# A retention layer with a gated convolution on one core: queries of six batches loaded four tokens to a partition, keys and queries turned apart, one load queue, and a new order in the slot

## The chip, the cores and the metric

The kernel runs on one NeuronCore of a Trainium2 chip. The metric is the device time of one execution in microseconds. PE is the matrix engine, DVE the vector engine, ACT the scalar engine, POOL the GpSimd engine and SP the sync engine, which here only issues transfers. SBUF is the on-chip memory, PSUM the small memory that PE writes; here PSUM is full, with eight banks of 2 KB per partition all in use.

## The reference

```python
def _attn_ref(q, k, v):                      # q, k, v: (8, 8, 576, 64) float32
    B, H, S, D_ = q.shape
    scores = 1.0 / np.sqrt(D_) * np.matmul(q, k.transpose(0, 1, 3, 2))
    gamma = 1.0 - 2.0 ** (-5.0 - np.arange(H, dtype=np.float32))
    rel = np.arange(S)[:, None] - np.arange(S)[None, :]
    Dmat = np.where(rel >= 0, gamma[:, None, None] ** rel[None, :, :], 0.0)
    return np.matmul(scores * Dmat[None], v)

def _moe_ref(x, w_val, conv_w, w_out):       # x: (8, 576, 512); conv_w: (5, 512)
    K = conv_w.shape[0]
    xp = np.concatenate([np.zeros((B, K - 1, D), np.float32), x], axis=1)
    gate_pre = sum(conv_w[k][None, None, :] * xp[:, k:k + S, :] for k in range(K))
    gate = 1.0 / (1.0 + np.exp(-gate_pre))
    return ((gate * (x @ w_val)) @ w_out).astype(np.float32)
```

The result of the attention, with the heads put side by side, is the `x` of the second part. There is no softmax: the decay `gamma ** (i - j)` splits into a factor for the key and one for the query, so a running state of keys times values can stand for all earlier tokens.

## The kernel before

**Tiling.** A batch has 576 tokens: four full chunks of 128 and a tail of 64. The list `chunks` holds 36 of them: for each group of four batches, sixteen full chunks, and then two tail chunks which pair the tails of two batches. Two chunks that follow each other make one unit of 256 tokens, and there are 18 units.

**One chunk.** `load` brings k, q and v by three transfers of 256 KB from SP, 64 floats (256 bytes) at a piece. `cast` on POOL makes bfloat16 copies `kb`, `qb` and, multiplied by the key's decay factor, `vb`. `turn` (L199) transposes `kb` and `qb` by PE into one PSUM tile `tps`, of which there is one; DVE copies the keys out (`kt`, L208), ACT the queries (`qt`, L209). `scores` (L220) multiplies them per head into two PSUM tiles, `masks` (L229) applies the causal mask on DVE, `values` (L261) multiplies with `vb`, on top of what `carried` (L244) has put there from the running state, and `take_x` (L270) scales the result by the query's factor into `xg`. `update` (L289) adds the chunk's keys and values to the state in PSUM, and `take_state` (L300) copies it out on ACT for the next chunk.

**One unit.** `conv` (L322) is 40 small matmuls with diagonal weights, `gate` (L330) two sigmoids on ACT, `value` two sets of 8 matmuls (L337), each with a product by the gate on DVE (`z`, L340), and `project` two sets of 4 matmuls (L347), each with a copy on ACT (`ob`, L350) and a transfer to the result from SP. These six PSUM tiles take turns in three banks, `g`.

**Order.** Nothing is reordered by a scheduler: each engine's instructions stand in the order in which the code is run through, with semaphores between engines. The loop runs over slots t = -2 to 37. Slot t loads chunk t+6, casts chunk t+4, turns chunk t+2, makes the scores of chunk t+1 and the values of chunk t. An even slot also runs `conv`, `gate` and `value` of unit t/2 - 1, the following odd slot its `project`. An engine thus waits at the first instruction whose input is not there, with all that is behind it. At most nine chunks of loads and four of casts are held at a time. The weights are loaded by ACT's queue, while SP loads the first chunks.

Of the kernel before, what the change touches and what calls it, by code (L numbers as in the profile page):

```python
# [13 lines left out]
F32 = mybir.dt.float32  # L14
# [7 lines left out]
def kernel(  # L22
# [20 lines left out]
    LA = 8  # L43
    assert D == 64 and DM == H * D and TAIL == 64 and B % GB == 0 and NP == 4
# [9 lines left out]
    op_sb = ctx.enter_context(tc.tile_pool(name="osb", bufs=3))  # L54
# [15 lines left out]
    with tc.manual_schedule():  # L70
# [3 lines left out]
        def load_chunk(b, c):  # L74
            for name, src in (("k", k), ("q", q), ("v", v)):
                t = half.tile([P, H, D], F32, name=f"f{name}c", bufs=LA + 1)
                nc.sync.dma_start(out=t, in_=src[b, :, c * P:(c + 1) * P, :].rearrange("h p d -> p h d"))  # L77
                loaded[name, "full", b, c] = t

        def load_tail(b):  # L80
            for name, src in (("k", k), ("q", q), ("v", v)):
                t = half.tile([P, H, D], F32, name=f"f{name}c", bufs=LA + 1)
                for i in range(2):
                    nc.sync.dma_start(out=t[i * TAIL:(i + 1) * TAIL],
                                      in_=src[b + i, :, NCH * P:S, :].rearrange("h p d -> p h d"))
                loaded[name, "tail", b, NCH] = t

        def load(t):
            kind, b, c = chunks[t]
            if kind == "full":  # L90
                load_chunk(b, c)
            else:
                load_tail(b)

        load(0)
        load(1)

        cwn = consts.tile([KC * NP, P], F32, name="cwn")
        nc.scalar.dma_start(out=cwn, in_=moe_conv_w.rearrange("k (o i) -> (k o) i", i=P))
        wvf = consts.tile([P, NP, DM], F32, name="wvf")  # L100
        wof = consts.tile([P, NP, DM], F32, name="wof")
        nc.scalar.dma_start(out=wvf, in_=moe_w_val.rearrange("(o i) n -> i o n", i=P))
        load(2)
        wo_src = moe_w_out.rearrange("(pr ab hl p) n -> ab hl p pr n", pr=2, ab=2, hl=2)
        for (p0, blk, ab, hl) in ((0, 0, 0, 0), (64, 0, 1, 0), (0, 2, 1, 1), (64, 2, 0, 1)):
            nc.scalar.dma_start(out=wof[p0:p0 + 64, blk:blk + 2, :], in_=wo_src[ab, hl])
# [3 lines left out]

        ident = consts.tile([P, P], BF16, name="ident")
# [3 lines left out]
        identf = consts.tile([32, 32], F32, name="identf")  # L115
        nc.vector.tensor_copy(identf, ident[0:32, 0:32])
# [5 lines left out]
        mask_t = consts.tile([P, P], BF16, name="maskt")  # L122
        nc.vector.tensor_copy(mask_t, mask)
        nc.vector.memset(mask_t[0:64, 64:128], 0.0)

        lrow = consts.tile([P, H], F32, name="lrow")
        lcol = consts.tile([P, NP], F32, name="lcol")
        for h in range(H):
# [302 lines left out]
```

## Time and profile before

| | us |
|---|---|
| median of 3 runs (range) | 194.98 (194.31 to 196.57) |
| the profiled execution | 196.09 |
| its span, first to last instruction | 194.1 |
| start of `conv` of unit 0, 2 and 16 | 29.29, 49.98, 178.22 |
| PE busy in the span | 152.2 (78%) |
| DVE, ACT, POOL busy | 114.3, 89.3, 86.9 |
| read from memory, written to it | 30.42 MB, 9.44 MB |

The profile tells for one execution when each engine worked, and what ended each idle time. It has three parts: a start until unit 2, in which data arrive; fourteen units from 49.98 to 178.22 that look alike; and an end, in which the last two units run without new chunks. The groups of instructions give a mean duration, which serves as the price of one instruction. The chain of waits goes back from the last instruction to what released it. The profiled execution took 1.1 us more than the median, of which 2.0 us lie outside the span.

### The profile page before, as it was taken

Reading aid. Unit: us, or ns where it says so; the run is one execution under the profiler, and the core shown is the slowest. Engines: PE = TensorE matmul, PEld = TensorE weight load, DVE = VectorE, ACT = ScalarE, POOL = GpSimd, SP = SyncE. Lnnn points to the kernel's source line nnn. Section 1 sums busy time; section 2 is a strip of 40 time slices with the busy share of each in tenths; the row PEclk is TensorE's granted clock in tenths of the full one; section 3 lists DMA queues with packets and bytes.
Section 4 is the critical chain, followed back from the end, with each engine's and each line's share of the span. In section 5 each row is a group of like instructions: output and inputs, shape, how many; then the busy total and the mean of one; then the engine's idle time right before and its main releaser. Section 6 shows DMA issues by size and latency. Waiting matters only on the chain.

```text
span 194.1 us, 5639 instructions
## 1 busy us (share of the span) xinstructions
PE 152.2 (78%) x2273; PEld 111.0 (57%) x2273; DVE 114.3 (59%) x211; ACT 89.3 (46%) x183; POOL 86.9 (45%) x126
## 2 busy tenths in 40 slices
PE   0112666998898989898988899788989898979990
PEld 0001545775666676667766576666666666667740
DVE  6406774747475657575766657474766575747420
ACT  0072635354646454444435464446463535354431
POOL 8214685655454626453644534454445362520000
PEclk9999999699999999999999999999999999999997
DMA  5999999999999999799999795999997998931124
GB/s 136 287 205 163 220 223 182 234 221 200 256 250 238 247 230 255 158 243 216 277 193 281 169 282 127 231 231 280 233 237 187 245 253 187 237 142 62 52 105 108
DMA packets 118919, 40.21 MB, mean 207 GB/s; under 512 B 113242, under 2 KB 113262, under 8 KB 118894
## 3 DMA queue, kind: packets, MB, share of 16 engines
q1 hardware_dynamic: 117760, 37.76, 86.3%
q10 hardware_dynamic: 1134, 2.11, 4.2%
q8 instruction: 17, 0.28, 0.7%
q14 instruction: 8, 0.07, 0.1%
HBM read 30.42 MB, written 9.44 MB: 205 GB/s over the span
## 4 chain that ended last, share of the span: by engine, by line
PE 48%; DMA 18%; ACT 12%; DVE 9%; SPq 4%; issue 4%; POOL 1%; ACTq 0%; DVEq 0%; POOLq 0%
PE g L337 10%; PE g L347 9%; PE g L322 9%; DMA fvc<-in_v_dram 7%; ACT qt L209 6%; DMA out_dram<-ob 5%; DMA fkc<-in_k_dram 5%; PE tps L205 5%; PE s L220 5%; PE o L261 4%; ACT gate L330 4%; PE st L289 4%; DVE kt L208 4%; DVE p L229 3%; SPq L77 2%
## 5 line engine op out<-in xcount | busy, mean ns | idle before, releaser
L229 DVE TENSOR_TENSOR p<-s,mask 128x512 bf16<-128x512 f32 x64 | 43.7, 684 | 19.3 <-PE s L220 19.3
L337 PE MATMUL g<-xg,wvb 128*128 128x256 bf16 x288 | 37.1, 272 | 14.7 <-ACT gate L330 13.4
L193 POOL TENSOR_TENSOR vb<-fvc,gin 128x512 bf16<-128x512 f32 x36 | 37.5, 1043 | 22.2 <-DMA fvc<-in_v_dram 16.0
L340 DVE TENSOR_TENSOR z<-gate,g 128x512 bf16<-128x512 f32 x36 | 24.8, 688 | 33.4 <-ACT gate L330 24.7
L337 PEld LDWEIGHTS <-wvb 128*128 128x128 bf16 x288 | 27.3, 97 | 21.1 <-issue 18.3
L191 POOL CAST kb<-fkc 128x512 bf16<-128x512 f32 x36 | 22.9, 636 | 31.9 <-DMA fkc<-in_k_dram 21.1
L192 POOL CAST qb<-fqc 128x512 bf16<-128x512 f32 x36 | 22.2, 617 | 29.4 <-DMA fqc<-in_q_dram 29.2
L347 PE MATMUL g<-wob,z 128*128 128x512 bf16 x144 | 34.4, 380 | 0.3 <-DVE z L340 0.3
L209 ACT COPY qt<-tps 128x512 bf16<-128x512 bf16 x36 | 21.1, 585 | 26.8 <-DVE kt L208 25.6
L350 ACT COPY ob<-g 128x512 f32<-128x512 f32 x36 | 21.0, 589 | 19.7 <-DMA out_dram<-ob 14.1
L300 ACT CAST sbd<-st 64x256 bf16<-64x256 f32 x48 | 17.6, 367 | 25.2 <-PE st L289 24.7
L322 PE MATMUL g<-xg,dg 64*64 64x256 bf16 x720 | 23.2, 271 | 0.0
L208 DVE COPY kt<-tps 128x512 bf16<-128x512 bf16 x36 | 15.1, 421 | 11.8 <-PE tps L205 11.7
L270 DVE TENSOR_TENSOR xg<-o,gout 128x512 bf16<-128x512 f32 x32 | 21.8, 681 | 0.0
L347 PEld LDWEIGHTS <-z 128*128 128x128 bf16 x144 | 13.3, 99 | 13.7 <-DVE z L340 1.2
L205 PE MATMUL tps<-ident,kb 128*128 128x128 bf16 x144 | 14.9, 229 | 7.1 <-POOL kb L191 7.1
L330 ACT ACTIVATE gate<-g 128x512 f32<-128x512 f32 x36 | 19.6, 601 | 1.7 <-PE g L322 1.7
L322 PEld LDWEIGHTS <-dg 64*64 64x64 bf16 x720 | 18.4, 106 | 2.0 <-issue 0.4
L205 PE MATMUL tps<-ident,qb 128*128 128x128 bf16 x144 | 14.9, 229 | 5.7 <-POOL qb L192 5.7
L220 PE MATMUL s<-qt,kt 64*128 64x128 bf16 x288 | 15.0, 225 | 4.5 <-ACT qt L209 4.3
L220 PEld LDWEIGHTS <-kt 64*128 64x128 bf16 x288 | 10.1, 96 | 10.2 <-DVE kt L208 4.1
L261 PE MATMUL o<-p,vb 128*64 128x128 bf16 x288 | 15.4, 230 | 0.0
(45 smaller groups left out, 108.1 us busy)
## 6 DMA issues: line engine op xcount, KB each, us to landing
fkc<-in_k_dram SPq DMA_DIRECT2D x32, 256.0 KB, 5.0
fqc<-in_q_dram SPq DMA_DIRECT2D x32, 256.0 KB, 5.3
fvc<-in_v_dram SPq DMA_DIRECT2D x32, 256.0 KB, 4.8
out_dram<-ob SPq DMA_DIRECT2D x32, 256.0 KB, 3.8
wvf<-in_moe_w_val_dram ACTq DMA_DIRECT2D x1, 1024.0 KB, 9.7
wof<-in_moe_w_out_dram ACTq DMA_DIRECT2D x4, 256.0 KB, 10.5
fkc<-in_k_dram SPq DMA_DIRECT2D x8, 128.0 KB, 3.4
fqc<-in_q_dram SPq DMA_DIRECT2D x8, 128.0 KB, 3.3
```

Of the source, the lines that this page charges most:

```text
L191: nc.gpsimd.tensor_copy(kb, loaded["k", kind, b, c])
L193: nc.gpsimd.tensor_tensor(vb, loaded["v", kind, b, c], gin[:, c, :].unsqueeze(2).to_broadcast([P, H, D]), op=ALU.mult)
L205: nc.tensor.transpose(ps[:, i, pr, :], flat[:, pr * P:(pr + 1) * P], ident)
L209: nc.scalar.copy(qt, ps[:, 1])
L220: nc.tensor.matmul(s[i][:, pr, :], lhsT=kt[r, pr, :], rhs=qt[r, pr, :], start=(pr == 0), stop=(pr == NP - 1), skip_group_check=True)
L229: nc.vector.tensor_tensor(p, sps[t][i], m.unsqueeze(1).to_broadcast([P, NP, P]), op=ALU.mult)
L261: nc.tensor.matmul(o[r, pr, :], lhsT=vb[:, 2 * pr + i, :], rhs=pt[t, i][:, pr, :], start=(fresh and pr == 0), stop=(pr == NP - 1), skip_gr ...
L322: nc.tensor.matmul(g[bank][cols, pr, :], lhsT=dg[rows, blk, kk, :], rhs=xs(n, rows, blk, kk), start=(pr == 0 and kk == 0), stop=(pr == 1 a ...
L330: nc.scalar.activation(t, gps[n][i], AF.Sigmoid)
L337: nc.tensor.matmul(vps[:, j, :], lhsT=wvb[:, o, 2 * i + j, :], rhs=xs(n, slice(0, P), o, PAD), start=(j == 0 and o == 0), stop=(j == 1 and ...
L340: nc.vector.tensor_tensor(z, gsb[n][i], vps, op=ALU.mult)
L347: nc.tensor.matmul(o, lhsT=zsb[n, j // 2][:, j % 2, i * P:(i + 1) * P], rhs=wob[:, j, :], start=(j == 0), stop=(j == NP - 1))
```

## The change

It has five pieces.

1. Of batches 2 to 7, the queries of the four full chunks come by one transfer of 1 MB (`load_queries`). Partition p holds tokens 4p to 4p+3, so that a piece is 1024 bytes long. A transposition of one of the four token positions r gives 128 columns for tokens r, r+4, r+8 and so on. ACT writes them with a step of four elements into a tile `qtb` of the whole batch, in which they stand in token order again. The queries of batches 0 and 1 and of all tails are loaded as before ("own").
2. `turn` is split into `turn_k` and `turn_q`, each with its own PSUM tile of half the size, from the same single buffer. A table `qjobs` deals the query jobs to slots: an own job two slots ahead of its chunk, a batch's four jobs one by one to the free slots before the batch begins. Slots 2, 3 and 4 hold two jobs each, and slots 29 to 31 and 34 onwards none. `cast_q` stands two slots ahead of its `turn_q`.
3. The weights `wvf` and `wof` move to SP's queue, between chunks 1, 2 and 3; ACT's queue keeps only the small `cwn`.
4. The constants before the loop are made in another order and partly on other engines: the zeroing of `sbd`, `sbl` and `xg` moves from POOL to DVE, `mask_t` from DVE to POOL into slot 2, the first two casts of k to DVE. The table for the sigmoid is loaded ahead by a one-column `warm`, and the diagonals and `wob` are made in four pieces each.
5. The order in a slot is new: `take_state` comes first, the two `gate` right behind `conv`, `turn_q` between the two halves of `value` or `project`, and `update` of the next chunk at the end. In odd slots `take_x` and the second mask come behind the copy of the keys. `ob` has five buffers instead of three.

The core of the diff:

```diff
-    op_sb = ctx.enter_context(tc.tile_pool(name="osb", bufs=3))
+    op_sb = ctx.enter_context(tc.tile_pool(name="osb", bufs=5))
...
+        def load_queries(b):
+            t = half.tile([P, H, RQ, D], F32, name="fqb", bufs=2)
+            nc.sync.dma_start(out=t.rearrange("p h r d -> p h (r d)"),
+                              in_=q[b, :, 0:RQ * P, :].rearrange("h (p r) d -> p h (r d)", r=RQ))
+            loaded["qb", b] = t
...
-        nc.scalar.dma_start(out=wvf, in_=moe_w_val.rearrange("(o i) n -> i o n", i=P))
+        nc.sync.dma_start(out=wvf, in_=moe_w_val.rearrange("(o i) n -> i o n", i=P))
...
+        def turn_q(job, eng=None):
+            ps = turned(qbf[job])
+            if job[0] == "own":
...
+                b, r = job[1:]
+                if r == 0:
+                    qtd["batch", b] = tp_sb.tile([P, NP, RQ * P], BF16, name="qtb", bufs=2)
+                dst = qtd["batch", b].rearrange("p o (n r) -> p o r n", r=RQ)[:, :, r, :]
+            if eng is nc.vector:
+                nc.vector.tensor_copy(dst, ps)
+            else:
+                nc.scalar.copy(dst, ps)
...
+            for b in qload.get(t, []):
+                load_queries(b)
             if t >= 0 and ok(t + LA - 2):
                 load(t + LA - 2)
+            for job in qjobs.get(t + 2, []):
+                cast_q(job)
             if ok(t + 4):
-                cast(t + 4)
+                cast_kv(t + 4)
+            if ok(t):
+                take_state(t)
             if ok(t + 1):
                 scores(t + 1)
                 masks(t + 1, 0)
             if ok(t):
                 values(t)
-                take_x(t)
-            if ok(t + 1):
+                if not odd:
+                    take_x(t)
+            if ok(t + 1) and not odd:
                 masks(t + 1, 1)
             if unit and not odd:
                 conv(n)
...
+                gate(n, 0)
+                gate(n, 1)
             if ok(t + 2):
-                turn(t + 2)
+                turn_k(t + 2)
+            if ok(t) and odd:
+                take_x(t)
+            if ok(t + 1) and odd:
+                masks(t + 1, 1)
...
+            if unit:
+                project(n, 0) if odd else value(n, 0)
+            for i, job in enumerate(jobs):
+                if i == 1 and unit:
+                    project(n, 1) if odd else value(n, 1)
+                turn_q(job, nc.vector if t < 0 else None)
+            if unit and len(jobs) < 2:
+                project(n, 1) if odd else value(n, 1)
             if ok(t + 1):
                 carried(t + 1)
+                update(t + 1)
```

The table `qload` puts the transfers of the batches 2 and 3 into slots 0 and 1, ahead of the loads of chunks 6 and 7, and those of batches 4 to 7 into slots 5, 11, 15 and 19.

How the instructions move is seen at three places. The first is ACT in slots 20 and 21 (unit 9), before. `sbd` and `sbl` are the copies of the state, `qt` or `qtb` the turned queries, `ob` the result's tile.

```order
L300 CAST sbd_187<-st 64x4x64 x2
L209 COPY qt<-tps 128x512
L330 ACTIVATE gate_2310<-g 128x512
L330 ACTIVATE gate_2312<-g 128x512
L300 CAST sbl_189<-st 64x4x64 x2
L209 COPY qt<-tps 128x512
L350 COPY ob<-g 128x512 x2
```

The same stretch of the changed kernel:

```order
L340 CAST sbd_184<-st 64x4x64 x2
L370 ACTIVATE gate_2321<-g 128x512
L370 ACTIVATE gate_2323<-g 128x512
L244 COPY qtb<-tps 128x512
L340 CAST sbl_186<-st 64x4x64 x2
L390 COPY ob<-g 128x512
L244 COPY qtb<-tps 128x512
L390 COPY ob<-g 128x512
```

The queries' copy stood ahead of the two gates; it now stands behind both, and in the odd slot between the two result copies.

The second place is DVE in slot 13 and the even slot 14, before: masks `p`, the taking of `xg`, the keys' copy `kt`, and the products `z`.

```order
L229 TENSOR_TENSOR p_1558<-s_1548,mask 128x512
L270 TENSOR_TENSOR xg_199<-o,gout 128x4x128
L229 TENSOR_TENSOR p_1569<-s_1549,mask 128x512
L208 COPY kt<-tps 128x512
L229 TENSOR_TENSOR p_1633<-s_1623,mask 128x512
L270 TENSOR_TENSOR xg_199<-o,gout 128x4x128
L229 TENSOR_TENSOR p_1644<-s_1634,mask 128x512
L208 COPY kt<-tps 128x512
```

And in the changed kernel, the same two slots:

```order
L269 TENSOR_TENSOR p_1595<-s_1585,mask 128x512
L227 COPY kt<-tps 128x512
L310 TENSOR_TENSOR xg_196<-o,gout 128x4x128
L269 TENSOR_TENSOR p_1613<-s_1586,mask 128x512
L269 TENSOR_TENSOR p_1668<-s_1658,mask 128x512
L310 TENSOR_TENSOR xg_196<-o,gout 128x4x128
L269 TENSOR_TENSOR p_1679<-s_1659,mask 128x512
L227 COPY kt<-tps 128x512
```

In the odd slot the keys' copy moved from the end to behind the first mask; in the even slot it stays behind both masks.

The third place is POOL at the casts of chunks 4 and 5, before; the numbers tell the tiles apart (`fkc_129` and `fkc_135` hold the keys of chunks 4 and 5):

```order
L191 CAST kb_288<-fkc_129 128x512
L192 CAST qb_289<-fqc_131 128x512
L193 TENSOR_TENSOR vb_290<-fvc_133,gin_175 128x512
L191 CAST kb_349<-fkc_135 128x512
L192 CAST qb_350<-fqc_137 128x512
L193 TENSOR_TENSOR vb_351<-fvc_139,gin_175 128x512
```

And in the changed kernel, where `fqb_290` is the tile of batch 2's queries:

```order
L212 CAST qb_298<-fqc_131 128x512
L212 CAST qb_300<-fqb_290 128x512
L197 CAST kb_302<-fkc_129 128x512
L198 TENSOR_TENSOR vb_303<-fvc_133,gin_164 128x512
L212 CAST qb_366<-fqc_137 128x512
L212 CAST qb_368<-fqb_290 128x512
L197 CAST kb_370<-fkc_135 128x512
L198 TENSOR_TENSOR vb_371<-fvc_139,gin_164 128x512
```

The cast of the first quarter of batch 2's queries (`fqb`, which needs the 1 MB transfer) now stands ahead of the cast of chunk 4's keys.

196 lines of the change are left out of this document (116 added, 80 removed).

## The prediction

> **What bounds the kernel now.** I read first the page's head and its queues, to see which resource could be full, then the busy time by stretches, with the stretches cut at the starts of `conv` of units 2 and 16, and then the waits within the long middle stretch.
>
> ```profile
> span 194.1 us, 5639 instructions
> q1 hardware_dynamic: 117760, 37.76, 86.3%
> q10 hardware_dynamic: 1134, 2.11, 4.2%
> PE 48%; DMA 18%; ACT 12%; DVE 9%; SPq 4%; issue 4%; POOL 1%; ACTq 0%; DVEq 0%; POOLq 0%
> ```
>
> Two things are nearly full: the transfers (the queues' packets fill 86.3 + 4.2% of the 16 engines' time) and PE, which leads the chain of waits with 48%. The stretches say which of the two sets the pace. Their columns are length, busy time of PE, PEld, DVE, ACT and POOL, the granted PE clock, the transfers' share and GB/s.
>
> ```profile
> 34.00:58.20 24.20, 22.17 (x300) 15.98 (x300) 15.32 (x26) 11.45 (x26) 13.84 (x19) 0.93 1.11 232
> 49.98:178.22 128.24, 114.52 (x1777) 84.74 (x1780) 81.54 (x143) 64.15 (x137) 59.57 (x79) 1.00 0.93 219
> 178.22:194.10 15.88, 10.62 (x146) 6.85 (x144) 5.05 (x10) 4.70 (x9) 0.00 (x0) 0.94 0.33 100
> ```
>
> The middle stretch holds 14 units in 128.24 us, 9.16 us each. PE is busy for 114.52 of it, 8.18 us a unit, and idle for 13.7 us. The transfers' share is 0.93, 119.3 us. Who ends PE's idle time there (total us, times, longest):
>
> ```profile
> PE g L337 <- ACT gate L330: 10.5, 14, 0.8
> PE s L220 <- ACT qt L209: 1.8, 6, 0.5
> PE g L337 <- ACT ob L350: 1.1, 2, 0.8
> ACT ob L350 <- DMA out_dram<-ob: 14.1, 11, 2.5
> ```
>
> Three waits make 13.4 of the 13.7 us. The chain through one unit shows them in place (start, length, what).
>
> ```profile
> 58.30 0.40 PE s L220 x8
> 58.69 0.34 PE o L261 x8
> 59.04 1.22 PE g L322 x40
> 60.59 0.46 PE tps L205 x8
> 61.07 0.44 DVE kt L208
> 61.53 0.59 ACT qt L209
> 62.12 0.51 ACT gate L330
> 62.66 1.03 PE g L337 x8
> 64.92 0.45 PE tps L205 x8
> 65.37 1.73 PE g L347 x8
> 67.10 0.22 PE o L244 x4
> 67.35 0.40 PE s L220 x8
> ```
>
> The second half of `value` needs the bank that the first gate empties. That gate stands behind the queries' copy, and that behind the keys' copy: it ends at 62.6, 2.4 us after `conv` has ended at 60.26. An undisturbed unit takes 67.35 - 58.30 = 9.05 us. PE and its partners set the pace; loads delay it only now and then, where `ob` waits for its transfer.
>
> **The new order in the slot.** The prices of what stands beside PE:
>
> ```profile
> L229 DVE TENSOR_TENSOR p<-s,mask 128x512 bf16<-128x512 f32 x64 | 43.7, 684 | 19.3 <-PE s L220 19.3
> L340 DVE TENSOR_TENSOR z<-gate,g 128x512 bf16<-128x512 f32 x36 | 24.8, 688 | 33.4 <-ACT gate L330 24.7 <-PE g L337 8.7
> L270 DVE TENSOR_TENSOR xg<-o,gout 128x512 bf16<-128x512 f32 x32 | 21.8, 681 | 0.0
> L208 DVE COPY kt<-tps 128x512 bf16<-128x512 bf16 x36 | 15.1, 421 | 11.8 <-PE tps L205 11.7
> L209 ACT COPY qt<-tps 128x512 bf16<-128x512 bf16 x36 | 21.1, 585 | 26.8 <-DVE kt L208 25.6
> L350 ACT COPY ob<-g 128x512 f32<-128x512 f32 x36 | 21.0, 589 | 19.7 <-DMA out_dram<-ob 14.1 <-issue 4.6 <-PE g L347 0.8
> ```
>
> I walk once through two slots with the new order. PE's pieces from the chain: scores 0.40, values 0.34, `conv` 1.22, one transposition 0.23 (half of 0.46), half a `project` 0.86, half a `value` as much (8 matmuls of 256 columns against 4 of 512), `carried` and `update` 0.22 each. The even slot takes 0.40 + 0.34 + 1.22 + 0.23 + 0.86 + 0.23 + 0.86 + 0.44 = 4.58 us, the odd slot, without `conv`, 3.36, the pair 7.94.
>
> Who would be late? After `conv`, at 1.96, ACT has nothing ahead of the gates, so the first ends at about 1.96 + 0.55; `value`'s second half starts at 3.28, and the wait of 10.5 us in 14 is gone. On DVE in the even slot the first mask can start at 0.47, then 0.684 + 0.681 + 0.684 + 0.421 put the keys' copy at 2.94; the queries' transposition, which needs the same `tps`, is due at 3.05. In the odd slot, the product `z` of the slot before ends 0.25 in, the mask starts at 0.47, and the copy ends at 1.57, against 1.83. The spare time is thus 0.1 and 0.26 us: enough, but thin. The queries' copy in the even slot ends near 3.9, long before the next transposition. It is also no longer what the next scores wait for, as a batch's queries are turned slots ahead: the 1.8 us go. With five `ob` the copy has two more transfers' time, and the 1.1 us go. The masks are due before the next scores by 0.4 us.
>
> The copy into `qtb` writes with a step of four elements, which no row shows. From below, it is the 0.585 of the plain copy; from above, I take twice that. Both lie beside PE: in the even slot it would end at 4.5, and the next transposition starts at 5.3. I take 0.585.
>
> So the pace falls to between 8.05 us (9.05 less the waits of 0.76 and 0.25 in the chain's unit) and the 8.18 of PE's busy time, and I add a little for new handoffs: 8.22. Over 14 units 115.0, a gain of 13.2 us. Bounds: 15.5 (8.05), and for the other end see the transfers.
>
> **The transfers.** The mean packet of q1 takes 0.863 x 16 x 194.1 / 117760 = 22.8 ns; nearly all are of 256 bytes. One of q10, mostly of 2 KB, takes 0.042 x 16 x 194.1 / 1134 = 115 ns. A packet of 1 KB is in no row. By bytes between these two it takes 62 ns; bounds are 57 (half of 115) and 91 (four small ones). About 22 of the 24 batched chunks' queries load in the middle stretch: 22 x 1024 x 22.8 / 16 = 32.1 us of the 119.3, which become 21.9. That leaves 109.1, under PE's 115.0. At 91 ns it stays 119.3, above it; that is a rival. The page "DMA: Bandwidth & Descriptors" of the Trainium skill (section "Why small descriptors are slow") gives a 256-byte piece 11 cycles, 3 of them overhead, so that 1 KB would save a fifth, not the third taken here; by it, as an estimate, a packet would take 72 ns, the middle stretch would still fit, and the 1 MB transfer in the start would cost 0.6 us more. No row here shows which holds.
>
> POOL casts as much as before. The transfer of batch 4's queries waits on SP until POOL has cast batch 2's last quarter, with chunk 11's loads queued behind; that cast stands one slot earlier, and chunk 11 is needed four slots later. I cost it at nothing; if late, the cover is those slots.
>
> **The start.** Here the change gives and takes.
>
> ```profile
> 1.92 9.00 ACTq L106 DMA_DIRECT2D wof<-in_moe_w_out_dram  x4
> 28.34 0.61 POOL L191 CAST kb<-fkc 128x512 bf16<-128x512 f32 x1 [0.24 <-DMA fkc<-in_k_dram]
> 29.50 0.62 POOL L192 CAST qb<-fqc 128x512 bf16<-128x512 f32 x1 [0.55 <-DMA fqc<-in_q_dram]
> 34.57 1.04 POOL L193 TENSOR_TENSOR vb<-fvc,gin 128x512 bf16<-128x512 f32 x1 [0.24 <-DMA fvc<-in_v_dram]
> 30.84 0.46 PE tps L205 x8
> 49.98 1.22 PE g L322 x40
> ```
>
> Issuing `wof` held ACT for 9.00 us, so the constants and the first copies came late. That goes, but buys little: from chunk 2 on the loads bound, one landing each 1.17 us (28.34 to 29.50). And POOL must now cast a quarter of batch 2's queries before chunk 4's keys; those queries are queued behind chunks 0 to 5 and the weights. I put it together: first bytes at 2.3 (issue at 0.80 and an estimate of 1.5), 18 loads of 1.17 = 21.1, the weights' 1024 packets at 115 ns, 7.4, the queries' 1024 at 62 ns, 4.0: 34.8. With packets a quarter faster, since those of the row shared the engines with another queue, it is 32.0. I take 33.4. The upper bound is what before had landed at 34.57, the same loads and weights, with the queries behind at 91 ns: 40.4.
>
> Casting the quarter and the keys takes 0.62 + 0.64, so chunk 4 is turned at 34.7, where before it was at 30.84. From there PE runs without waiting: the rest of slot 2 (2.9, with its second job), slot 3 (3.6), slot 4 (4.8), slot 5 (3.4) and 0.74 to the next `conv`: 15.4 us. By the same count chunk 3 has landed at 23.7, and slot 2 runs for 2 us before it needs chunk 4, so PE has been idle for some 9 us. It starts at a lower clock: the stretch from 34.00 shows 0.93 granted, 24.2 x 0.07 = 1.7 us lost, after a spell of waiting. The page "TensorE: Matmul & The Clock Gate" (section "What's actually happening") says that an idle window of about 3.4 us halves the clock and a busy one restores it; the row agrees, and the rule speaks against this order at this place. With 1.7, `conv` of unit 2 starts at 51.8 instead of 49.98: 1.8 later, with bounds of -1.3 (32.0, and no clock lost) and +8.8 (40.4). I put 2.1, as the second jobs lengthen these slots' handoffs too.
>
> The end, 15.88 us, has no turning, and its order is the same but for the gates; I leave it. What moves among the constants lies before chunk 2's landing.
>
> **Sum.** 196.1 - 13.2 + 2.1 = 185.0 for the profiled execution. It stands 1.1 above the median of 194.98: 184 us.
>
> **The rivals.** The transfers become the bound. Against it: 0.93 in the middle at a pace set by PE, with 10 us of PE's waits on ACT. For it: at 91 ns nothing is saved. Then 119.3 us of transfers, with the 0.98 that a full stretch may reach, take 121.7; the gain is 6.5, and the 1 MB transfer in the start takes 1.8 more: 196.1 - 6.5 + 3.9 - 1.1 = 192.4.
>
> The split turning waits instead: slower. One `tps` now passes PE, DVE, PE, ACT twice in a slot. DVE's spare times are 0.1 and 0.26. If DVE runs one mask (0.684) behind, PE stands still before `turn_q` for 0.58 and 0.42, and the unit takes 8.22 + 1.0 = 9.22; 14 of them are 129.1. That gives 196.1 + 0.9 + 2.1 - 1.1 = 198.0. It decides once the copy of the keys ends more than 0.5 us a slot behind the first half of `value`. Against it: DVE is busy for 81.54 of 128.24 us, and would be for 71% of the new pace.
>
> The start is cheaper and the pace is 8.05: 196.1 - 15.5 - 1.3 - 1.1 = 178.2. Or the change in the queries' load does nothing and the old waits return elsewhere, with no more gained than the start loses: 195.
>
> **How the numbers follow.** The forecast has a chance of 0.60, the transfers 0.17, better than forecast 0.09, the split turning 0.08, no effect 0.06. The measurement can't tell changes under 1% from none: 193.0 to 196.9. Faster by more: 0.60 + 0.09 + 0.13 of the transfers' case = 0.82; within 1%: 0.06 + 0.04 = 0.10; slower 0.08. The range goes from the better case to the transfers' case: 178 to 192.5; outside lie the split turning, no effect, and small parts of the others.
>
> **What would show it.** PE's wait for the gate gone in the middle, and `conv` to `conv` at about 8.2 us; no idle time of PE before `turn_q` released by the keys' copy; q1 at some 100000 packets, with the weights' now among them; chunk 4's keys cast right after the first quarter of batch 2, at about 34 us, with PE idle before. The prediction is wrong if PE's idle time in the middle stays over 5 us, if POOL there waits longer for loads than now, or if unit 2's `conv` starts before 49 or after 56.

## The result, and the profile after

The kernel after takes 185.94 us (median of 4 runs, 184.13 to 186.75), the kernel before 195.77 in the same sessions (4 runs, 194.31 to 198.53). The ratio is 0.9509, with a 95% interval of 0.9397 to 0.962: faster, by close to a twentieth. The ratios here and below leave out executions more than 1.5% longer than the fastest of the same kernel, and the medians keep them. Its profiled execution took 186.13 us, with a span of 184.1.

The page of the kernel after, head, queues and the chain by engine:

```profile
span 184.1 us, 5545 instructions
q1 hardware_dynamic: 100144, 39.86, 91.3%
PE 61%; SPq 17%; DVE 7%; ACT 7%; DMA 3%; issue 2%; POOL 0%; DVEq 0%; ACTq 0%
```

PE's share of the chain went from 48% to 61%, and the queue has 17,600 packets fewer, although it now carries the weights too. The busy time by stretches, cut at the same places as for before (the starts of `conv` of units 2 and 16); columns as there:

```profile
0.00:56.60 56.60, 30.56 (x375) 22.63 (x381) 27.48 (x76) 24.28 (x43) 25.63 (x45) 0.94 1.05 227
56.60:167.62 111.02, 109.61 (x1746) 83.63 (x1764) 83.81 (x143) 75.77 (x132) 54.15 (x74) 1.00 0.95 234
167.62:184.10 16.48, 10.37 (x144) 6.86 (x144) 5.06 (x10) 4.51 (x8) 0.00 (x0) 0.94 0.29 86
```

So the 10.0 us between the two spans are a middle that is 17.2 shorter (128.24 to 111.02, now 7.93 a unit), a start that is 6.6 longer (49.98 to 56.60) and an end that is 0.6 longer. In the middle PE is idle for 1.4 us, where it was for 13.7, and half of the 1.4 lies before `project`, of which the trace lacks 14 matmuls. The waits there, of PE, ACT and POOL:

```profile
PE s L260 <- ACT qtb L244: 0.3, 1, 0.3
ACT gate L370 <- PE g L362: 9.2, 14, 1.5
POOL kb L197 <- DMA fkc<-in_k_dram: 15.5, 6, 4.1
POOL qb L212 <- DMA fqc<-in_q_dram: 11.6, 4, 4.6
POOL vb L198 <- DMA fvc<-in_v_dram: 8.8, 13, 2.3
```

The first row is all that PE waits for. ACT now waits for `conv` before a gate, where `value` waited for the gate. POOL waits 35.9 us for loads, without PE noticing. The chain through one unit shows the new order at work:

```profile
71.92 0.33 PE s L260 x8
72.25 0.34 PE o L301 x8
72.59 1.22 PE g L362 x40
73.81 0.33 PE tps L219 x4
74.14 0.87 PE g L377 x8
75.02 0.24 PE tps L219 x4
75.28 1.31 ACT qtb L244
76.63 0.39 PE s L260 x7
...
79.88 0.33 PE s L260 x8
```

From scores to scores it takes 7.96 us (71.92 to 79.88), almost all of it PE. The keys' transposition, half a `value` and the queries' transposition follow `conv` without a gap, where before PE waited for the gate. The row of ACT lies beside PE's second half of `value`, and the next scores start right behind it.

What the start lost shows on POOL (start, length, what, and in brackets the idle time before it):

```profile
16.68 0.61 POOL L212 CAST qb<-fqc 128x512 bf16<-128x512 f32 x1 [5.51 <-DMA fqc<-in_q_dram]
24.81 0.61 POOL L212 CAST qb<-fqc 128x512 bf16<-128x512 f32 x1 [5.96 <-DMA fqc<-in_q_dram]
28.51 0.61 POOL L212 CAST qb<-fqc 128x512 bf16<-128x512 f32 x1 [1.44 <-DMA fqc<-in_q_dram]
37.51 0.61 POOL L212 CAST qb<-fqb 128x512 bf16<-128x512 f32 x1 [8.38 <-DMA fqb<-in_q_dram]
38.06 0.61 POOL L197 CAST kb<-fkc 128x512 bf16<-128x512 f32 x1
```

These are the queries of chunks 2, 3 and 4, then the first quarter of batch 2, and right behind it the keys of chunk 4. Those keys stand on the queue ahead of chunk 4's queries, which were cast at 28.51; their cast stood in POOL's order behind a quarter that landed at 37.5. PE waited for them:

```profile
38.73 0.61 PE L219 MATMUL tps<-ident,kb 128*128 128x128 bf16 x4 [6.71 <-POOL kb L197]
39.13 1.91 PE L377 MATMUL g<-xg,wvb 128*128 128x256 bf16 x8
49.38 1.04 PE L377 MATMUL g<-xg,wvb 128*128 128x256 bf16 x8
```

### The profile page after: what moved, and what is told of

It reads as the page before. It is cut to its first block, busy times and chain, and to the rows that moved or that the text cites. A ratio compares the mean times of both kernels' runs of the same rounds, so it can differ in the third digit from the quotient of the medians.

```text
span 184.1 us, 5545 instructions
## 1 busy us (share of the span) xinstructions
PE 150.5 (82%) x2255; PEld 113.1 (61%) x2273; DVE 116.3 (63%) x227; ACT 104.6 (57%) x182; POOL 79.8 (43%) x118
## 3 DMA queue, kind: packets, MB, share of 16 engines
q1 hardware_dynamic: 100144, 39.86, 91.3%
## 4 chain that ended last, share of the span: by engine, by line
PE 61%; SPq 17%; DVE 7%; ACT 7%; DMA 3%; issue 2%; POOL 0%; DVEq 0%; ACTq 0%
PE g L387 16%; PE g L377 15%; SPq L79 14%; PE g L362 11%; PE tps L219 8%; ACT qtb L244 6%; DVE p L269 5%; PE s L260 5%; PE o L301 4%; DMA fqc<-in_q_dram 3%; DVE z L380 3%; PE st L329 2%; SPq L109 1%; PE o L284 1%; SPq L95 1%
## 5 line engine op out<-in xcount | busy, mean ns | idle before, releaser
L269 DVE TENSOR_TENSOR p<-s,mask 128x512 bf16<-128x512 f32 x64 | 43.9, 685 | 16.2 <-PE s L260 15.1
L198 POOL TENSOR_TENSOR vb<-fvc,gin 128x512 bf16<-128x512 f32 x36 | 37.5, 1042 | 14.1 <-DMA fvc<-in_v_dram 10.6
L377 PE MATMUL g<-xg,wvb 128*128 128x256 bf16 x288 | 38.1, 278 | 0.0
L390 ACT COPY ob<-g 128x512 f32<-128x512 f32 x36 | 22.2, 618 | 24.6 <-PE g L387 24.6
L244 ACT COPY qtb<-tps 128x512 bf16<-128x512 bf16 x24 | 31.5, 1314 | 5.0 <-PE tps L219 5.0
L387 PE MATMUL g<-wob,z 128*128 128x512 bf16 x126 | 32.9, 379 | 1.4 <-DVE z L380 0.5
L197 POOL CAST kb<-fkc 128x512 bf16<-128x512 f32 x34 | 20.8, 613 | 28.3 <-DMA fkc<-in_k_dram 15.5
L219 PEld LDWEIGHTS <-kb 128*128 128x128 bf16 x144 | 8.9, 102 | 25.8 <-POOL kb L197 15.5
L362 PE MATMUL g<-xg,dg 64*64 64x256 bf16 x720 | 24.2, 279 | 0.0
L212 POOL CAST qb<-fqc 128x512 bf16<-128x512 f32 x12 | 7.3, 610 | 30.1 <-DMA fqc<-in_q_dram 28.4
L212 POOL CAST qb<-fqb 128x512 bf16<-128x512 f32 x24 | 14.6, 610 | 8.5 <-DMA fqb<-in_q_dram 8.4
L244 ACT COPY qt<-tps 128x512 bf16<-128x512 bf16 x10 | 5.9, 588 | 17.9 <-PE tps L219 17.9
```

The lines of the kernel that those rows point to most:

```text
L198: nc.gpsimd.tensor_tensor(vb, loaded["v", kind, b, c], gin[:, c, :].unsqueeze(2).to_broadcast([P, H, D]), op=ALU.mult)
L212: nc.gpsimd.tensor_copy(qb, src)
L219: nc.tensor.transpose(ps[:, pr, :], flat[:, pr * P:(pr + 1) * P], ident)
L244: nc.scalar.copy(dst, ps)
L269: nc.vector.tensor_tensor(p, sps[t][i], m.unsqueeze(1).to_broadcast([P, NP, P]), op=ALU.mult)
L362: nc.tensor.matmul(g[bank][cols, pr, :], lhsT=dg[rows, blk, kk, :], rhs=xs(n, rows, blk, kk), start=(pr == 0 and kk == 0), stop=(pr == 1 a ...
```

## The experiments

Two questions were open. Which part of the change gave the middle its 17.2 us, the order in the slot or the cheaper transfers? And what did the start's 6.6 us pay for: could the same middle be had without them? In the table, "start" ends and "end" begins at the same two `conv` as above (us, of the one profiled execution of each). Executions with the same loads differ in the start by up to 1.9 us (56.60, 54.93 and 54.71 for the kernel after and the two experiments that don't touch its loads), so a start is read to about 2 us. The profiled execution of e3 took 194.79 us, somewhat more than its median, and is used only to see where a wait went.

| kernel | median, us | ratio to before (95%) | start | middle |
|---|---|---|---|---|
| before | 195.77 | 1 | 49.98 | 128.24 |
| after | 185.94 | 0.9509 (0.9397–0.962) | 56.60 | 111.02 |
| e1, batch 2's queries later | 183.04 | 0.9373 (0.9313–0.9432) | 48.08 | 116.94 |
| e2, every batch loaded the old way | 187.27 | 0.961 (0.954–0.9681) | 45.40 | 122.78 |
| e3, before with gates first | 194.25 | 0.9859 (0.9805–0.9913) | – | – |
| e4, plain copy into `qtb` | 183.52 | 0.9424 (0.9348–0.9501) | 54.93 | 109.94 |
| e5, three `ob` | 188.78 | 0.9723 (0.9622–0.9824) | 54.71 | 115.53 |
| e6, before with gates first and five `ob` | 187.94 | 0.9651 (0.9523–0.9779) | 47.69 | 120.84 |
| e7, e1 with batches 4 to 7 later | 183.96 | 0.948 (0.9378–0.9582) | 47.47 | 119.91 |
| e8, 2 KB pieces everywhere | 176.70 | 0.906 (0.8926–0.9195) | 44.86 | 111.04 |
| e9, e1 with the step in PE's read | 204.23 | 1.0478 (1.0421–1.0536) | 47.92 | 137.43 |
| e10, weights on ACT's queue | 187.81 | 0.9584 (0.9501–0.9668) | 59.12 | 111.03 |
| e11, three own batches, step in the read | 199.74 | 1.0226 (1.0178–1.0275) | 45.59 | 136.45 |
| e12, three own batches | 183.54 | 0.9414 (0.9345–0.9482) | 46.66 | 117.79 |

**e1: batch 2's queries later.** In the kernel after, the four query jobs of batch 2 move to slots 4, 5, 6 and 6, their transfer stands behind chunk 6's loads, batch 3's two slots later, and a batch's quarter is cast behind the slot's keys and values.

```diff
+        qjobs = {s: [j for j in js if j[:2] != ("batch", 2)] for s, js in qjobs.items()}
+        for s, r in ((4, 0), (5, 1), (6, 2), (6, 3)):
+            qjobs.setdefault(s, []).append(("batch", 2, r))
...
-            qload.setdefault(max(0, s0 - LA + 2), []).append(b)
+            qload.setdefault({2: 1, 3: 3}.get(b, s0 - LA + 2), []).append(b)
...
-                cast_q(job)
+                if job[0] == "own":
+                    cast_q(job)
...
+            for job in qjobs.get(t + 2, []):
+                if job[0] != "own":
+                    cast_q(job)
```

> Change: the changed kernel, with batch 2's query transfer moved behind chunk 6's loads and batch 3's behind chunk 8's, batch 2's four query jobs in slots 4, 5, 6 and 6, and a batch's query cast behind the casts of keys and values in its slot. Theory A (the 1 MB transfer ahead of chunk 4's key cast cost the start): chunk 4's keys are turned near 30 us instead of 38.7, conv of unit 2 starts at about 50 instead of 56.6, and the time falls by 5 to 7 us, to about 180. Rival B (the transfers as a whole bind by now, with a share of 1.05 in the start and 0.95 in the middle): conv of unit 2 starts earlier, but the middle stretch grows from 111 us to 114 or more, POOL waits for loads there, and the time falls by less than 3 us.

Measured: 183.04 us. The start is 8.5 us shorter than after's, so the early place of that transfer was the start's loss; but 5.9 of it come back in the middle. The start is as theory A has it, with chunk 4's keys turned at 31.23; the middle (116.94, where B has 114 or more) and the time (2.9 us less by the medians, where B has less than 3) are rival B's. The stretches, and the place on POOL that gives most of it back:

```profile
0.00:48.08 48.08, 28.82 (x371) 21.19 (x371) 27.92 (x76) 22.33 (x40) 22.35 (x40) 1.00 1.10 229
48.08:165.02 116.94, 112.48 (x1764) 84.37 (x1760) 83.90 (x143) 77.65 (x135) 57.61 (x79) 0.99 0.97 238
```

```profile
87.74 0.61 POOL L212 CAST qb<-fqc 128x512 bf16<-128x512 f32 x1 [5.96 <-DMA fqc<-in_q_dram]
```

POOL stands for 5.96 us before the queries of a tail, with keys queued behind; the `conv` around it are 11.98 us apart (81.85 and 93.83) where a unit takes 7.93. The transfers' share of the middle is 0.97.

**e2: every batch loaded the old way.** The kernel after with no 1 MB query loads, so the new order in the slot stands by itself (with five `ob` and one queue).

```diff
-    FIRST = 2
+    FIRST = B
```

> Change: the changed kernel with the queries of all batches loaded as before, in pieces of 256 bytes, one transfer per chunk; the slot order, the one load queue and the split turning stay. Theory A (without the pieces of 1 KB the transfers bind): conv of unit 2 starts near 50 us, the middle stretch takes 119 to 122 us with a transfer share near 1, and PE waits for POOL's casts there; the time is about 188. Rival B (the slot order alone sets the pace): the middle stays at 111 us and the time is about 179.

Measured: 187.27 us. It is theory A for the middle, where the transfers bind; the start is shorter than the 50 us expected. The queue on the page, the middle stretch, and the waits in it:

```profile
q1 hardware_dynamic: 118864, 39.86, 100.1%
```

```profile
45.40:168.18 122.78, 111.69 (x1772) 83.79 (x1768) 83.94 (x143) 64.08 (x135) 59.19 (x81) 1.00 1.06 236
```

```profile
POOL qb L212 <- DMA fqc<-in_q_dram: 58.7, 27, 3.1
PE tps L219 <- POOL kb L197: 10.9, 13, 1.4
```

The queue is full, POOL waits 58.7 us for queries, and PE 10.9 us for POOL. The batched loads take the middle from 122.78 to 111.02, 11.8 us; but the start is 11.2 us shorter without them (45.40 against 56.60). Unit 16's `conv` is at 168.18 here and at 167.62 in the kernel after. As the change places them, the batched loads bought 0.6 us net in these two executions and 1.3 by the medians, and the intervals of the two ratios overlap. Against the kernel before, e2's start is 4.6 us shorter (45.40 against 49.98); which of the other pieces gave that is not shown. The converse, the batched loads in the old order, was not run.

**e3: the gates first, in the kernel before.** One line moved, to ask how much the removed wait of 10.5 us is worth alone.

```diff
             conv(n)
+                gate(n, 0)
+                gate(n, 1)
...
-                gate(n, 0)
-                gate(n, 1)
                 value(n, 0)
```

> Change: the kernel before, with one thing moved: the two gates stand right behind conv, ahead of the copy of the turned queries on ACT. Theory A (the gate behind the queries' copy was the main wait): PE's wait for the gate, 10.5 us in the middle stretch, goes; the middle falls from 128 to about 118 to 120 us and the time by 7 to 10 us, to 186 to 188. Rival B (the wait moves to the queries' copy, now behind two gates, or to the loads): the middle stays above 125 us and the time within 2% of before.

Measured: ratio 0.9859 (0.9805 to 0.9913, 10 runs), 1.4%, about 2.8 us, as the rival has it. The wait was not worth what it was long. In its profiled execution, one of its longer ones, PE waits for no gate there any more, and in its place stands

```profile
PE g L337 <- ACT ob L350: 11.1, 12, 3.2
```

PE waits 11.1 us for `ob`, where it was 1.1 in the profile before.

**e6: the same with five `ob`.**

```diff
-    op_sb = ctx.enter_context(tc.tile_pool(name="osb", bufs=3))
+    op_sb = ctx.enter_context(tc.tile_pool(name="osb", bufs=5))
```

> Change: the kernel before with two things: the two gates right behind conv, and five buffers for the result's tile. Theory A (moving the gates alone only let PE's wait pass to the result's buffers): the middle falls from 129 us to 119 to 123, where the transfers bind, and the time to 186 to 189. Rival B (the transfers or the turning of keys and queries in one go bind already): the middle stays above 126 us and the time above 192.

Measured: ratio 0.9651 (0.9523 to 0.9779), which is theory A. With all other parts of the change left out, these two edits give 3.5% of its 4.9%, some seven tenths of the gain, with overlapping intervals. The middle stretch, and what POOL and PE wait for in it now:

```profile
47.69:168.53 120.84, 113.17 (x1764) 84.07 (x1774) 81.93 (x143) 63.59 (x137) 60.51 (x80) 1.00 1.05 235
```

```profile
POOL kb L191 <- DMA fkc<-in_k_dram: 21.4, 15, 2.6
PE tps L205 <- POOL qb L192: 5.2, 11, 1.0
```

No row of `gate` or `ob` is left among PE's waits; PE waits for POOL and POOL for loads. Whether the slot is ordered the old way (120.84) or the new (e2's 122.78), with queries in 256-byte pieces the middle stops at about 121 to 123 us, where the transfers are full (shares of 1.05 and 1.06).

**e5: three `ob` in the kernel after.**

```diff
-    op_sb = ctx.enter_context(tc.tile_pool(name="osb", bufs=5))
+    op_sb = ctx.enter_context(tc.tile_pool(name="osb", bufs=3))
```

> Change: the changed kernel with three buffers for the result's tile instead of five. Theory A (the result's transfers stand in the queue behind loads, and with three buffers ACT, and behind it PE, wait for them): ACT's wait for out_dram comes back with over 10 us, PE waits for the result's copy, the middle grows by 4 to 8 us and the time to 189 to 193. Rival B (the buffers don't matter once the slot order is new): the time stays within 1 us of the changed kernel's.

Measured: 188.78 us, ratio 0.9723 (0.9622 to 0.9824), just clear of after's interval: 2.8 us by the medians, and 4.5 in the middle (115.53). That is theory A, but ACT's wait is shorter than the 10 us it expected. The waits for `ob` return in the middle:

```profile
ACT ob L390 <- DMA out_dram<-ob: 6.2, 5, 3.8
PE g L377 <- ACT ob L390: 2.5, 1, 2.5
```

One of them stops PE for 2.5 us, and around it two `conv` are 12.1 us apart (86.71 and 98.82). Buffers whose lack seemed to cost 1.1 us of waits in the profile before are worth 2.8 to 4.5 at the new pace.

**e4: the step out of the copy.** The kernel after writes the queries' columns side by side into `qtb`, so its tokens stand in another order than the reference's; the work is the same but for the step.

```diff
-                dst = qtd["batch", b].rearrange("p o (n r) -> p o r n", r=RQ)[:, :, r, :]
+                dst = qtd["batch", b][:, :, r * P:(r + 1) * P]
```

> Change: the changed kernel with the turned queries written side by side instead of with a step of four elements, so that the queries of batches 2 to 7 stand in the wrong token order (all instructions and sizes stay). Theory A (the step of four makes the copy 1.31 us instead of 0.59, but it lies beside PE): the copy falls to about 0.59 us and the time stays within 1 us of the changed kernel's. Rival B (the copy, 5.7% of the chain of waits, holds the next turning of keys in the one PSUM buffer): the middle falls by 4 us or more.

Measured: 183.52 us, ratio 0.9424 (0.9348 to 0.9501), which overlaps after's. By the medians it is 2.4 us faster, more than the 1 us of theory A; 1.7 of it lies in the start (54.93), whose loads are the same. The copies in the kernel after, the one with the step and below it the one without (busy time in all, mean ns of one):

```profile
L244 ACT COPY qtb<-tps 128x512 bf16<-128x512 bf16 x24 | 31.5, 1314 | 5.0 <-PE tps L219 5.0
L244 ACT COPY qt<-tps 128x512 bf16<-128x512 bf16 x10 | 5.9, 588 | 17.9 <-PE tps L219 17.9
```

The step more than doubles the copy, 17.4 us of ACT in all (24 x 0.726), and taking them away shortens the middle by 1.1 (111.02 to 109.94), far from the rival's 4: they lie beside PE.

**e9: the step in PE's read instead.** On top of e1, columns written side by side and PE picking every 128th of them for a chunk (a step of 256 bytes).

```diff
-                dst = qtd["batch", b].rearrange("p o (n r) -> p o r n", r=RQ)[:, :, r, :]
+                dst = qtd["batch", b][:, :, r * P:(r + 1) * P]
...
-            return qtd["batch", b][:, :, c * P:(c + 1) * P]
+            w = P // RQ
+            return qtd["batch", b].rearrange("p o (r n) -> p o n r", r=RQ)[:, :, c * w:(c + 1) * w, :]
```

> Change: the kernel with batch 2's queries loaded later, and the turned queries written side by side, while PE reads them with a step of 128 elements, so that the tokens stand in order in the scores. Theory A (the reading costs PE nothing, and the copy of 0.59 instead of 1.31 us gives what it gave alone): the scores' matmuls stay at 216 to 220 ns, and the time falls by 1 to 2 us below the 183.0 of the kernel with the later queries. Rival B (PE reads slower with a step): the scores' and carried matmuls of batches 2 to 7 grow by over 30 ns each, and the time is 185 or more.

Measured: 204.23 us, slower than the kernel before by 4.8%. That is the rival, and more strongly than put:

```profile
L261 PE MATMUL s<-qtb,kt 64*128 64x128 bf16 x192 | 24.8, 388 | 0.2 <-ACT qtb L244 0.2
L285 PE MATMUL o<-qtb,sbd 128*128 128x128 bf16 x72 | 18.6, 392 | 0.0
```

The same scores without the step, from e1:

```profile
L260 PE MATMUL s<-qtb,kt 64*128 64x128 bf16 x192 | 9.6, 218 | 1.5 <-ACT qtb L244 1.2
```

The step costs nothing on ACT, which has time, and 15.2 us on the scores alone, on PE, which has none. The change put it on the right side.

**e8: the same bytes in long pieces.** The kernel after with every full chunk's k, v and own queries read from contiguous memory, 2 KB a piece. The tokens and heads are then other ones than the reference's; the instructions are the same.

```diff
-                nc.sync.dma_start(out=t, in_=src[b, :, c * P:(c + 1) * P, :].rearrange("h p d -> p h d"))
+                nc.sync.dma_start(out=t.rearrange("p h d -> p (h d)"),
+                                  in_=src[b].rearrange("h s d -> (h s d)")[c * P * DM:(c + 1) * P * DM]
+                                  .rearrange("(p x) -> p x", x=DM))
```

> Change: the changed kernel with every load of a full chunk (k, v, and the queries that are loaded by chunk) taken from the same number of bytes that lie side by side, in pieces of 2 KB instead of 256 bytes, so that the tokens in a tile are the wrong ones; the work on them is the same. Theory A (the start is bound by the transfers, the middle by PE): chunk 4's keys are turned near 27 us, conv of unit 2 starts at 44 to 46 instead of 56.6, the middle stays within 2 us of 111, and the time falls to 174 to 177. Rival B (the transfers hold the middle too): the middle falls below 107 us and the time below 172.

Measured: 176.70 us, ratio 0.906 (0.8926 to 0.9195). That is theory A.

```profile
0.00:44.86 44.86, 29.03 (x372) 21.57 (x374) 27.77 (x76) 24.21 (x43) 25.55 (x45) 1.00 0.97 321
44.86:155.90 111.04, 109.62 (x1748) 83.66 (x1758) 83.88 (x143) 75.89 (x132) 54.64 (x74) 1.00 0.71 220
```

The middle doesn't move (111.04), though the transfers' share falls from 0.95 to 0.71: there the kernel after is bound by PE. The start is 11.7 us shorter, with the batch's transfer in the same early place, and PE waits 1.68 us for chunk 4's keys instead of 6.71: what the start lost there was transfer time.

**e7: batches 4 to 7 later.** e1 with the 1 MB transfers of batches 4 to 7 four slots before the first of their own turnings, two slots later than in e1.

```diff
-            qload.setdefault({2: 1, 3: 3}.get(b, s0 - LA + 2), []).append(b)
+            qload.setdefault({2: 1}.get(b, s0 - 4), []).append(b)
```

> Change: the kernel with batch 2's queries loaded later, and the 1 MB query transfers of batches 3 to 7 too, four slots ahead of their first turning instead of six (batch 5's so comes behind the tails' loads). Theory A (the stop of PE before the first tails was a matter of the order on the queue): conv of unit 2 stays at 48 us, the stop of 4 us before unit 7 goes, the middle takes 112 to 114 us and the time is 178 to 180. Rival B (the transfers bind as a whole, whatever their order): the stop only moves, and the time stays at 182 to 184.

Measured: 183.96 us, no different from e1 within the intervals, as the rival has it. The longest stop now stands at 89.06 to 102.47 between two `conv`, and the middle is 119.91.

**e12 and e11: three batches loaded the old way.** In the kernel after, batch 2 is loaded chunk by chunk too, the later ones four slots ahead, a quarter cast behind the slot's keys and values. e11 also has e9's step in PE's read; e12 the change's step in the copy.

```diff
-    FIRST = 2
+    FIRST = 3
...
-            qload.setdefault(max(0, s0 - LA + 2), []).append(b)
+            qload.setdefault(s0 - 4, []).append(b)
...
```

> Change: as the kernel with the step in PE's reading, but with batch 2's queries loaded by chunk too, and the 1 MB transfers of batches 3 to 7 four slots ahead of their first turning. Theory A (the transfers bind as a whole, so that an early start is paid back by a later stop): conv of unit 2 starts near 46 us, PE stops for loads before or at the first tails for 3 us or more, and the time is 182 to 184. Rival B (only the place of the first 1 MB transfer mattered): no stop over 1 us, and the time is 178 to 180.

> Change: the changed kernel with batch 2's queries loaded by chunk too, the 1 MB transfers of batches 3 to 7 four slots ahead of their first turning, and a batch's query cast behind the casts of keys and values; the copy writes with a step of four as in the changed kernel, and PE reads side by side. Theory A (the transfers bind as a whole, so that an early start is paid back by a later stop): conv of unit 2 starts near 46 us, PE stops for loads for 3 us or more before unit 9, and the time is 182 to 184. Rival B (only the place of the first 1 MB transfer mattered): the middle stays under 113 us and the time is 176 to 180.

Measured: e11 199.74 us, which says nothing on the loads, as its middle (136.45) is that of e9's matmuls. e12 183.54 us, as theory A has it:

```profile
0.00:46.66 46.66, 28.14 (x361) 20.78 (x362) 28.33 (x76) 20.72 (x40) 19.54 (x35) 1.00 1.05 224
46.66:164.45 117.79, 113.47 (x1772) 84.62 (x1768) 83.96 (x143) 77.25 (x135) 60.76 (x84) 0.99 0.98 241
```

The start is 9.9 us shorter than after's, and the middle 6.8 longer. e1, e7 and e12 load the batches at three different paces, and end at 183.0, 184.0 and 183.5. In all three the early start is repaid by a stop in the middle (in e12 from 89.52 to 101.20 between two `conv`).

**e10: the weights on ACT's queue again.**

```diff
-        nc.sync.dma_start(out=wvf, in_=moe_w_val.rearrange("(o i) n -> i o n", i=P))
+        nc.scalar.dma_start(out=wvf, in_=moe_w_val.rearrange("(o i) n -> i o n", i=P))
...
-            nc.sync.dma_start(out=wof[p0:p0 + 64, blk:blk + 2, :], in_=wo_src[ab, hl])
+            nc.scalar.dma_start(out=wof[p0:p0 + 64, blk:blk + 2, :], in_=wo_src[ab, hl])
```

> Change: the changed kernel with the two weights loaded by ACT's queue again, all else as changed. Theory A (the same bytes must land before batch 2's queries, whoever issues them): the first query transfer of 1 MB still lands at 36 to 39 us, conv of unit 2 starts within 1.5 us of 56.6, and the time stays within 1% of the changed kernel's, though the first chunks land some us later. Rival B (one queue in order of need was worth something): the 1 MB transfer lands past 40 us and the time grows by 2 us or more.

Measured: 187.81 us, between the two expectations; its interval overlaps after's, so a gain of some 2 us from the one queue is not shown beyond doubt.

```profile
1.93 9.33 ACTq L109 DMA_DIRECT2D wof<-in_moe_w_out_dram  x4
39.87 0.62 POOL L212 CAST qb<-fqb 128x512 bf16<-128x512 f32 x1 [8.61 <-DMA fqb<-in_q_dram]
```

ACT is held for 9.33 us again, and the quarter of batch 2 comes 2.4 us later than in the kernel after (37.51), the middle being the same.

## Why the prediction was right, and where it was not

The time came out 1.9 us above the forecast of 184.0, well inside the range, and the direction is the one given 0.82. But two terms of the sum were off by 4.0 and 4.5 us, in opposite directions, so that the time came so close is luck. With the end's 0.6 they leave 1.1; the rest is that the profiled execution stood 0.2 above its median this time, where the sum took 1.1.

**The new order in the slot: mechanism right, size short.** PE's wait for the gate is gone, and the walk's 7.94 us for a pair of slots is what the chain shows (7.93 a unit over 14). The step that failed is the choice between them: the forecast held PE's busy 8.18 us a unit to be near a floor and took 8.22, and so 13.2 us for the middle instead of 17.2, which lies outside its own bound of 15.5. Busy time fell from 114.52 to 109.61 us, although the mean durations in the middle did not (`value` 272 ns, `project` 379). Of these 4.9 us, 0.9 is work that now lies in the start (in the middle, 100 matmuls that transpose queries against 112, and 100 of `update` against 104, at 0.22 us for four) and 0.7 the records that the trace lacks. The rest fits the waits: eight matmuls of `value` show 1.04 us, but what follows them without a wait starts after 0.87, so each of the 22 waits of PE in the middle of before adds some 0.17 of busy time, 3.7 us in all. That is an estimate. A busy time that includes the ends of interrupted runs of matmuls is no floor: in e4 PE is busy for all of the middle, 109.94 us, 7.85 a unit. The walk, made of pieces of the chain, was the better witness.

**The start: the mechanism right, two sizes wrong.** Batch 2's quarter did stand before chunk 4's keys, cast one right behind the other, and PE was idle. The quarter came at 37.5, where 33.4 was taken, 34.8 by the rows. The choice of "packets a quarter faster" is the first 1.4 us, and nothing here bears it out. Of the other 2.7, 2.4 had been lost by chunk 4's queries: 2.3 + 14 x 1.17 + 7.4 gives 26.1, and they were cast at 28.51. From there the four loads and the batch's megabyte took 9.0, against 4.7 + 4.0. Part of the 2.4 shows in an issue on SP's queue, and in the transfers' share of the first 40 us, in slices of 1 us and tenths:

```profile
10.13 4.42 SPq L79 DMA_DIRECT2D fvc<-in_v_dram  x1
```

```profile
DMA  0089999998999926999999999999999999999497
```

One load's issue held SP until 14.55, and in the slices of 14 and 15 us the engines are 0.28 and 0.67 busy: about 1 us of nothing to move. Why that issue took 4.42 us isn't known; the kernel before has one of 5.41 at 5.53, behind which the engines stay busy. Behind the landing the count was good: from chunk 4's turning to `conv` of unit 2 it takes 17.87 us (38.73 to 56.60), 17.1 were forecast. The sign "wrong if unit 2's `conv` starts after 56" was tripped, at 56.60, and rightly: the term was +6.6, not +2.1, though within its bounds. Taken apart by e2, the batched loads cost the start 11.2 us and the rest of the change gained 4.6.

**The clock.** After its wait PE's eight value matmuls take 1.91 us, at 39.13, where they take 1.04 at 49.38. The granted clock was 0.50 from 38.73 to 41.00, after 6.7 us of waiting, and 1.00 from 43.00 on. The stretch from chunk 4's turning to `conv` of unit 2 was granted 0.91 of the clock:

```profile
38.73:56.60 17.87, 17.11 (x226) 12.88 (x232) 10.41 (x18) 11.63 (x21) 14.26 (x22) 0.91 0.99 238
```

That is 1.6 us lost, where 1.7 was forecast from the stretch of before. It agrees with the Trainium skill's page "TensorE: Matmul & The Clock Gate", section "What's actually happening", which has an idle window halve the clock and a busy one restore it.

**The diagnosis was only half right.** "PE and its partners set the pace; loads delay it only now and then" failed as a price list. The three waits, 13.4 us of PE's idle time, were stacked and not side by side: without the gate's wait alone the kernel gains 1.4%, as PE then waits for `ob` (e3), with two more `ob` 3.5% (e6), and then loads bind at 120.84, close to the 119.3 of transfers that the prediction had worked out. To go below took the batched queries, 9.8 to 11.8 of the middle's 17.2 us (after against e6 and e2). The share of 0.93 in the profile before meant that a gain of more than some 5 to 7 us in the middle (to the 120.84 of e6 or the 122.78 of e2) had to come through the transfers. The sum had this condition, since it set 109.1 us of transfers under PE's 115, but not its price in the start. The 0.98 that the rival took for a full stretch was too low: e2 and e6 show 1.06 and 1.05.

**A packet of 1 KB** was put at 62 ns, bounds 57 and 91. e2's mean packet takes 1.001 x 16 x 184.1 / 118864 = 24.8 ns, and the 24,576 small packets of the batched queries so 38.1 us of 16 engines. The kernel after has 16.2 us less of packets' time (100.1% and 91.3% of 184.1), so its 6,144 large ones take 21.9 us, 57 ns each. But the mean holds 5,632 packets of 2 KB, results and weights. "Nearly all are of 256 bytes" is right by number (the page counts 113,242 of 118,919 under 512 bytes), not by time: at 115 ns each the others take a fifth. If a size costs the same in e2, the kernel after and e8 (72.7% of 172.4 us, for 14,640 small packets, 6,144 of 1 KB and 14,848 of 2 KB), the three queues together give some 21, 44 and 96 ns for 256 bytes, 1 KB and 2 KB. That is an estimate too, and by it even the lower bound was too high; the middle's transfers came to 105.5 us (0.95 of 111.02) instead of 109.1. The Trainium skill's page "DMA: Bandwidth & Descriptors" (section "Why small descriptors are slow") would by an estimate have had 72; the runs are on the other side.

**The step in the copy** was priced at 0.585, upper bound 1.17; it took 1.314. Its cover held: it costs 1.1 us in the middle (e4), and PE's two waits for it in the start, at 44.30 and 53.14, are 0.3 us each.

**The rivals.** That transfers would bind was wrong for the kernel after and right for e2 and e6; e1, e7 and e12 stop for loads too, with shares of 0.97, 0.94 and 0.98 in the middle. That the split turning would wait, the slower case, was rightly put low: PE waits for no copy of the keys in the middle, and for one of the queries once, 0.3 us. That the queries' load does nothing had 0.06 and is nearest to what e2 shows of that part taken alone, 0.6 us net, but not of the whole. The issue of `wof`, said to buy little by its going, may buy 2 us (e10).

**The end** was left at nothing and cost 0.6.

## What to carry to other kernels

Waits on the slowest engine can be stacked behind one another: before a wait is priced at its length, take the next resource's own time in that stretch (here the transfers' 119.3 us of 128.24) as the floor that the gain runs into. A transfer that is made large so as to be cheap also lands late as a whole, and whatever an in-order engine has queued behind its consumer waits with it; here the 1 MB loads saved 11.8 us in the middle and cost 11.2 in the start. And put a stepped access on the engine that has time.

## What was not expected of the hardware

ACT's copy of 128x512 bf16 from PSUM into a tile with a step of four elements, 8 bytes, took 1314 ns against 588 without it. PE's matmuls of 128 columns took 388 and 392 ns with a step of 256 bytes in the moving operand, 218 and 219 without. And one load's issue held SP for 4.42 us, and the engines ran short behind it, where the others of the same size in the first 45 us took 0.45 to 3.62.

What stays open: no run has the start of e12 and the middle of e8 with the reference's layout. e1, at 183.04 us, is the fastest of those that compute the reference; its interval reaches to 0.9432, after's begins at 0.9397, so its lead of 2.9 us is likely and not certain.
